# A gated causal convolution on one core: which load goes on which DMA queue at the start, and how the last left-over piece is evicted at the end

## The chip, the cores and the metric

The kernel runs on one core of one Trainium2 chip. The core has a matrix engine (TensorE, "PE" in the profile, with its weight loads as "PEld"), a vector engine (VectorE, "DVE"), a scalar engine (ScalarE, "ACT"), GpSimd ("POOL") and a queue engine (SyncE, "SP"). Transfers between the chip's memory and the core are issued here from two instruction streams, SP's and ACT's, and are carried out by 16 DMA engines. The metric is the device time of one execution in microseconds (us); 287.65 us is the median of three runs before the change.

## The reference

```python
B, T, D, K = (2, 16000, 256, 3)          # x: (B, T, D), w: (K, D, 2D), w_o: (D, D), all bf16
dil = 2
pad = (K - 1) * dil
xp = jnp.pad(x, ((0, 0), (pad, 0), (0, 0)))
h = jnp.einsum('btc,cd->btd', xp[:, pad:pad + T, :], w[0])
for i in range(1, K):
    off = pad - i * dil
    h = h + jnp.einsum('btc,cd->btd', xp[:, off:off + T, :], w[i])
f = h[..., :D]
g = h[..., D:]
z = jnp.tanh(f) * jax.nn.sigmoid(g)
return z @ w_o
```

Each output step t needs x at t, t-2 and t-4, each through its own 256 x 512 matrix ("tap" 0, 1, 2); half of the 512 results go through tanh, half through sigmoid, their product is `z` (called the gate below), and `z` goes through a 256 x 256 matrix.

## The kernel before

**Tiling.** Time is cut into rows of four steps (`j` = 0 to 3), 4000 rows per batch. Channels lie on the 128 partitions, in two halves `ct`. Rows are taken in 33 groups: 160 rows, then groups of 256 rows, and at the end 160, 128 and 128 rows. For each group there are four blocks of 128 output channels (`oi`, in the order of `O_ORDER`), so the main loop runs over `k = 4 * group + oi`, 132 steps. A step has two PSUM banks, `a` (steps 0 and 1 of each row) and `b` (steps 2 and 3).

**The two ways to form a step.** `direct` (L222) forms both banks tap by tap from the three weight matrices: 12 matmuls a step. It is used for the first group, steps 0 to 3, since it needs nothing but x and the taps. From step 4 on `products` (L201) needs 8 matmuls a step: two with mixed matrices `wm`, `wp` on a difference `mm` and a sum `pp` of x, two with tap 0 and two with tap 2 on differences `dd`. `weights` (L140) makes the mixed matrices: ACT halves tap 1 (L141), DVE adds taps 0 and 2 (L142) and forms `wm` and `wp` (L144). `pre_m`, `pre_p` and `pre_d` (L171, L177, L183) make `mm`, `pp` and `dd` on DVE and, for one quarter of group 1's `dd` and all later ones, GpSimd. `copy_m2` and `combine` (ACT L247, DVE L254 and L255) join the two banks, `activate` (ACT, L268) applies tanh or sigmoid, `gate` (DVE, L277) multiplies.

**Output.** `out_mm` (L281) multiplies a piece of `z` (up to 128 rows, two of the four steps of a row, called `jp` 0 or 1) by `w_o` into an `o_ps` bank of 128 x 512 values; `out_evict` (L295) copies that bank to the tile `osb` on ACT (L305) or, near the end, on DVE (L303), and after `jp` 1 issues the store of both `jp` from SP (L308). A piece is evicted one step after it was made (the list `made`), so one piece of the last but one group is left over when the loop ends: before the change it is evicted in the pass `k == NB`, on DVE, ahead of `finish`.

**The start.** The order is written out by hand. ACT's stream issues the load of tap 0 (`w0_sb`, L116) and then the load of its function table (L117). SP's stream issues x for the first 80 rows and the next 80 rows (L122, `xn0` and `xn1`, 160 KB each), then taps 1 and 2 (`w12_sb`, L126, 512 KB), then a transposing load of x for the second chunk (L104), the output matrix (L131) and another transposing load. PE meanwhile runs 24 matmuls on zeros (`warm_up`, L91), transposes `xn0` when it has landed (`turn(0)`, L155), runs 4 more zeros, transposes `xn1`, runs 4 zeros again and begins tap 0. `turn` copies each transposed half from PSUM to the tile `xt`, one half on DVE (L161), one on ACT (L163). The direct steps then run tap by tap: tap 0 of steps 0 to 2 (12 matmuls of 320 columns), tap 1, tap 2, and then step 3.

```python
    for tap in range(K):
        for k in range(3):
            direct(k, (tap,))
    weights()
```

**The end.** `finish` (L312) takes the last block of the last group: `activate`, two half gates (L322, first `jp` 1, then `jp` 0), and for each `jp` two banks of `z @ w_o` (L330); ACT copies the first bank (L335) and DVE the second (L337) to a tile `osb_end`, and SP stores it (L339).

Of the kernel before, what the change touches and what calls it, by code (L numbers as in the profile page):

```python
# [13 lines left out]
def kernel(  # L14
# [18 lines left out]
    nc = tc.nc  # L33
    bf16 = mybir.dt.bfloat16
    f32 = mybir.dt.float32
    B, T, D = x.shape
    K, _, D2 = w.shape
    P = 128
# [2 lines left out]
    NT = D // P  # L41
    RH = 16
    RG = 256
    N_WARM = (24, 4, 4)
    O_ORDER = (0, 2, 1, 3)
    FIRST = (160,)
    LAST = (128, 128)
# [40 lines left out]
    def warm_up(n):  # L88
        wps = ps_a.tile([P, 2 * RG], f32, name="a")
        for _ in range(n):  # L90
            nc.tensor.matmul(wps[:, :P], lhsT=warm[:], rhs=warm[:], start=True, stop=True)  # L91
# [20 lines left out]
    w0_sb = consts.tile([P, CT, D2], bf16)  # L112
    w12_sb = consts.tile([P, 2, CT, D2], bf16)
    wo_sb = consts.tile([P, NT, D], bf16)
    w_taps = [w0_sb, w12_sb[:, 0], w12_sb[:, 1]]
    nc.scalar.dma_start(out=w0_sb[:], in_=w[0].rearrange("(ct c) d -> c ct d", c=P))  # L116
    nc.scalar.preload_act_table(ACT.Sigmoid)  # L117
    warm_up(N_WARM[0])
    xns = []
    for i, (r0, r) in enumerate(TILES):  # L120
        xn = consts.tile([P, 4, D], bf16, name=f"xn{i}")
        nc.sync.dma_start(  # L122
            out=xn[:r], in_=x[0, 4 * r0:4 * (r0 + r), :].rearrange("(r j) c -> r j c", j=4)
        )
        xns.append(xn)
    nc.sync.dma_start(out=w12_sb[:], in_=w[1:3].rearrange("k (ct c) d -> c k ct d", c=P))  # L126
    ident = consts.tile([P, P], bf16)
    make_identity(nc, ident[:])
    for c in range(2):
# [18 lines left out]
    def turn(i):  # L148
        r0, r = TILES[i]
        for h in range(2):  # L150
            pool, tag = ((ps_o, "o_ps"), (ps_b, "b"))[i]
            tp = pool.tile([P, 2, CT, P], bf16, name="tp", tag=tag)
            for j in range(2):
                for ct in range(CT):
                    nc.tensor.transpose(  # L155
                        out=tp[:, j, ct, :r], in_=xns[i][:r, 2 * h + j, ct * P:(ct + 1) * P],
                        identity=ident[:r, :r],
                    )
            dst = xts[0][:, 2 * h:2 * h + 2, :, RH + r0:RH + r0 + r]
            if h == 0:  # L160
                nc.vector.tensor_copy(out=dst, in_=tp[:, :, :, :r])  # L161
            else:
                nc.scalar.copy(out=dst, in_=tp[:, :, :, :r])  # L163
# [7 lines left out]
    def pre_m(g):  # L171
        xp, yp, xc, yc = views(g)
        G = groups[g]
        G["m"] = m_pool.tile([P, 2, CT, RG], bf16, name="mm")
        return nc.vector.tensor_tensor(out=G["m"][:, :, :, :G["R"]], in0=xc, in1=yp, op=ALU.subtract)  # L175
# [25 lines left out]
    def products(k, which):  # L201
        g, oi = divmod(k, 4)
        G = groups[g]
        o = O_ORDER[oi]
        osl = slice(o * P, (o + 1) * P)
        R = G["R"]
        N = 2 * R
        if which in (1, 2):
            G["ab"[which - 1], oi] = (ps_a, ps_b)[which - 1].tile([P, 2 * RG], f32, name="ab"[which - 1])
        wmat, mv, bank, first = {  # L210
            2: (wm_sb, lambda ct: G["m"][:, :, ct, :R], "b", True),
            1: (wp_sb, lambda ct: G["p"][:, :, ct, :R], "a", True),
            3: (w_taps[0], lambda ct: G["d"][:, 2:4, ct, :R], "b", False),
            0: (w_taps[2], lambda ct: G["d"][:, 0:2, ct, :R], "a", False),
        }[which]
        for ct in range(CT):
            nc.tensor.matmul(  # L217
                G[bank, oi][:, :N], lhsT=wmat[:, ct, osl], rhs=mv(ct),
                start=first and ct == 0, stop=ct == CT - 1, skip_group_check=True,
            )  # L220
# [21 lines left out]
    def copy_m2(k):  # L242
        g, oi = divmod(k, 4)
        G = groups[g]
        N = 2 * G["R"]
        G["ss", oi] = ss_pool.tile([P, 2 * RG], f32, name="ss")
        nc.scalar.copy(out=G["ss", oi][:, :N], in_=G["b", oi][:, :N])  # L247
# [9 lines left out]
    def activate(k):  # L257
        g, oi = divmod(k, 4)
        G = groups[g]
        R = G["R"]  # L260
        o = O_ORDER[oi]
        if oi == 0:
            G["th"] = act_pool.tile([P, NT, 4, RG], bf16, name="th")
            G["sg"] = act_pool.tile([P, NT, 4, RG], bf16, name="sg")
            G["z"] = z_pool.tile([P, NT, 4, RG], bf16, name="zz")
        dst = G["th"][:, o] if o < NT else G["sg"][:, o - NT]
        for h, bank in ((1, "b"), (0, "a")):
            nc.scalar.activation(  # L268
                out=dst[:, 2 * h:2 * h + 2, :R],
                in_=G[bank, oi][:, :2 * R].rearrange("p (q r) -> p q r", q=2),  # L270
                func=ACT.Tanh if o < NT else ACT.Sigmoid,
            )
# [19 lines left out]
                    start=(dt == 0), stop=(dt == NT - 1),  # L292
                )

    def out_evict(g, rb0, jp, on_dve):  # L295
        G = groups[g]
        rn = min(P, G["R"] - rb0)
        ps = slice(rb0 - max(0, rb0 + rn - P), rb0 - max(0, rb0 + rn - P) + rn)
        if jp == 0:
            G["osb", rb0] = osb_pool.tile([P, 4, D], bf16, name="osb")  # L300
        osb, o_ps = G["osb", rb0], G["o", rb0, jp]
        if on_dve:
            nc.vector.tensor_copy(out=osb[ps, 2 * jp:2 * jp + 2, :], in_=o_ps[ps])  # L303
        else:
            nc.scalar.copy(out=osb[ps, 2 * jp:2 * jp + 2, :], in_=o_ps[ps])  # L305
        if jp == 1:
            t0 = 4 * (G["r0"] + rb0)
            nc.sync.dma_start(  # L308
                out=out[G["b"], t0:t0 + 4 * rn, :].rearrange("(p j) d -> p j d", j=4), in_=osb[ps]
            )  # L310

    def finish():  # L312

        g = NG - 1
        G = groups[g]
        R = G["R"]
        assert R <= P
        dt = NT - 1
        activate(4 * g + 3)
        for jp in (1, 0):  # L320
            js = slice(2 * jp, 2 * jp + 2)
            nc.vector.tensor_tensor(  # L322
                out=G["z"][:, dt, js, :R], in0=G["th"][:, dt, js, :R], in1=G["sg"][:, dt, js, :R], op=ALU.mult
            )
        for jp in (1, 0):
            osb = osb_pool.tile([P, 2, D], bf16, name="osb_end")
            for q in range(2):
                ps = (ps_a if q == 0 else ps_b).tile([P, 2 * RG], f32, name="ab"[q])
                for d in range(NT):
                    nc.tensor.matmul(  # L330
                        ps[:R, :D], lhsT=G["z"][:, d, 2 * jp + q, :R], rhs=wo_sb[:, d, :],
                        start=(d == 0), stop=(d == NT - 1),
                    )
                if q == 0:
                    nc.scalar.copy(out=osb[:R, q, :], in_=ps[:R, :D])  # L335
                else:
                    nc.vector.tensor_copy(out=osb[:R, q, :], in_=ps[:R, :D])  # L337
            t0 = 4 * G["r0"]
            nc.sync.dma_start(  # L339
                out=out[G["b"], t0:t0 + 4 * R, :].rearrange("(p j) d -> p j d", j=4)[:, 2 * jp:2 * jp + 2, :],  # L340
                in_=osb[:R],
            )
# [10 lines left out]
    NG = len(groups)  # L353
    NB = 4 * NG
    todo, made = [], []
    turn(0)
    warm_up(N_WARM[1])
    turn(1)
    warm_up(N_WARM[2])
    for tap in range(K):  # L360
# [21 lines left out]
    k = N_DIRECT + 1  # L382
    while k <= NB:
        g, oi = divmod(k, 4)
        if k < NB:
            products(k, 2)
            products(k, 1)
            copy_m2(k)
        products(k - 1, 3)
        products(k - 1, 0)  # L390

        for piece in made:
            out_evict(*piece, k == NB or g == NG - 1 and oi in (0, 2))
        made = []
        n = 1 if k < NB else 0
        while todo and todo[0][0] <= k and n:
            piece = todo.pop(0)[1]
            out_mm(*piece)
            made.append(piece)
            n -= 1  # L400

        if k < NB:
            combine(k)
        last = None
        if k < NB and oi == (1 if g == 1 else 0) and g + 1 < NG:
            last = pre_m(g + 1)
        elif k < NB and oi == 2 and g + 1 < NG:
            last = pre_p(g + 1)
        elif oi == 3 and g < NG:
            last = gate(g, 0)  # L410
        elif oi == 1 and 1 < g < NG:
            last = gate(g - 1, 1)
            drain(g - 1, k + 1)
        if k < NB and g + 1 < NG:
            pre_d(g + 1, oi, nc.gpsimd, last)
        if k < NB:
            activate(k - 1)

        if k < NB and oi == 3 and loaded < len(chunks) and groups[min(g + 1, NG - 1)]["chunk"] + 2 >= loaded:
            load_chunk(loaded)  # L420
            loaded += 1
        k += 1
    assert not todo and not made
    finish()


# [28 lines left out]
```

## Time and profile before

| what | us |
|---|---|
| median of three runs | 287.65 |
| lowest and highest of them | 287.0 and 288.33 |
| the profiled execution, its own time | 288.56 |
| span of the profiled execution, first to last instruction | 286.5 |
| PE busy in it | 281.1 |
| ACT busy in it | 261.1 |
| DVE busy in it | 241.8 |

All times of the trace count from the start of the span. The profiled execution is one run: its own time lies 0.91 us above the median and above the highest of the three. Start and length of an instruction are both printed; on ACT and DVE a following instruction can start a little before the one ahead has ended. Matmuls are printed by their start, and their ends are modelled. A name such as "ACTq" or "SPq" is the stream of instructions of that engine that issues transfers or waits for counters, as against the engine's own work. Of a transfer the profile has the time of its issue and the time until it has landed:

```
w_sb<-in_w_dram SPq DMA_DIRECT2D x1, 512.0 KB, 5.2
xn<-in_x_dram SPq DMA_DIRECT2D x2, 160.0 KB, 3.8
w_sb<-in_w_dram ACTq DMA_DIRECT2D x1, 256.0 KB, 4.1
xt<-in_x_dram SPq DMA_TRANSPOSE x2, 6.7
```

These are the issues in the first 15 us; the last number is the median from issue to landing.

### The profile page before, as it was taken

The numbers are of one execution on the slowest core, as the hardware profiler recorded it, in microseconds if no ns is written. First come the engines' busy times: TensorE is split into PE (matmuls) and PEld (weight loads), VectorE is DVE, ScalarE is ACT, GpSimd is POOL, SyncE is SP. The second block draws the span as 40 slices with busy tenths as digits, with TensorE's granted clock in tenths as the row PEclk, the third lists the DMA queues.
The fourth block names the chain that finished last, engine by engine and source line by source line (L and its number), as shares of the span: only waits on it lengthen the run. The fifth ranks groups of instructions, "written<-read, shape, count | busy, mean of one in ns | idle before, by whom it ended". The sixth has DMA issues, their size and how long they took to land.

```text
span 286.5 us, 4835 instructions
## 1 busy us (share of the span) xinstructions
PE 281.1 (98%) x1632; PEld 159.2 (56%) x1632; DVE 241.8 (84%) x401; ACT 261.1 (91%) x521; POOL 126.1 (44%) x133
## 2 busy tenths in 40 slices
PE   7999999999999999999999999999999999999994
PEld 6655555555555555555555555555555555555783
DVE  1788988888888888888888888888888888888885
ACT  3489999999999999999999999999999999999994
POOL 1134444454455455445445445445445544543430
PEclk9999999999999999999999999999999999999999
DMA  7908783561926429182371913718273251611222
GB/s 196 209 0 200 184 167 106 125 166 38 223 76 144 120 74 185 73 192 71 112 188 39 224 73 82 182 66 196 75 165 98 82 132 55 118 46 65 76 110 82
DMA packets 75767, 34.50 MB, mean 120 GB/s; under 512 B 66432, under 2 KB 67712, under 8 KB 75744
## 3 DMA queue, kind: packets, MB, share of 16 engines
q1 hardware_dynamic: 75472, 33.95, 46.3%
q8 instruction: 12, 0.20, 0.3%
q10 hardware_dynamic: 272, 0.26, 0.3%
q14 instruction: 11, 0.09, 0.1%
HBM read 1.25 MB, written 16.38 MB: 62 GB/s over the span
## 4 chain that ended last, share of the span: by engine, by line
PE 96%; DMA 2%; DVE 1%; issue 0%; SPq 0%; ACT 0%
PE b L217 37%; PE a L217 37%; PE o_ps L290 19%; DMA xn<-in_x_dram 2%; PE a L236 1%; PE b L236 1%; DVE osb_end L337 0%; PE tp L155 0%; DVE osb L303 0%; DVE a L255 0%; PE a L91 0%; DVE zz L277 0%; SPq L122 0%; ACT ss L247 0%; PE a L330 0%
## 5 line engine op out<-in xcount | busy, mean ns | idle before, releaser
L192 POOL TENSOR_TENSOR dd<-xt 128x512 bf16<-128x512 bf16 (+2 forms) x125 | 125.2, 1002 | 150.1 <-DVE zz L277 68.9
L254 DVE TENSOR_TENSOR b<-a,ss 128x512 f32<-128x512 f32 (+2 forms) x128 | 86.6, 676 | 35.2 <-ACT ss L247 32.7
L255 DVE TENSOR_TENSOR a<-a,ss 128x512 f32<-128x512 f32 (+2 forms) x128 | 85.3, 667 | 0.0
L247 ACT COPY ss<-b 128x512 f32<-128x512 f32 (+2 forms) x128 | 72.7, 568 | 12.5 <-PE b L217 0.9
L217 PEld LDWEIGHTS <-w_sb 128*128 128x128 bf16 x512 | 49.9, 98 | 55.9 <-DVE a L255 0.4
L290 PE MATMUL o_ps<-wo_sb,zz 128*128 128x256 bf16 x504 | 75.7, 273 | 0.0
L217 PE MATMUL a<-pp,wp_sb 128*128 128x512 bf16 (+2 forms) x256 | 73.8, 370 | 0.0
L217 PE MATMUL a<-dd,w_sb 128*128 128x512 bf16 (+2 forms) x256 | 73.8, 370 | 0.0
L217 PE MATMUL b<-mm,wm_sb 128*128 128x512 bf16 (+2 forms) x256 | 73.8, 370 | 0.0
L217 PE MATMUL b<-dd,w_sb 128*128 128x512 bf16 (+2 forms) x256 | 73.8, 370 | 0.0
L305 ACT CAST osb<-o_ps 128x512 bf16<-128x512 f32 (+1 forms) x123 | 72.9, 593 | 0.1
L290 PEld LDWEIGHTS <-zz 128*128 128x128 bf16 x504 | 49.1, 98 | 30.8 <-DVE zz L277 0.5
L268 ACT ACTIVATE th<-b 128x512 bf16<-128x512 f32 (+2 forms) x66 | 39.2, 594 | 3.9 <-PE b L236 3.8
L277 DVE TENSOR_TENSOR zz<-th,sg 128x1024 bf16<-128x1024 bf16 (+2 forms) x65 | 42.7, 658 | 0.0
L217 PEld LDWEIGHTS <-wp_sb 128*128 128x128 bf16 x256 | 25.0, 98 | 27.9
L268 ACT ACTIVATE sg<-b 128x512 bf16<-128x512 f32 (+2 forms) x66 | 39.3, 595 | 0.5 <-PE b L236 0.4
L268 ACT ACTIVATE sg<-a 128x512 bf16<-128x512 f32 (+2 forms) x66 | 39.3, 596 | 0.0
L268 ACT ACTIVATE th<-a 128x512 bf16<-128x512 f32 (+2 forms) x66 | 39.3, 595 | 0.0
L217 PEld LDWEIGHTS <-wm_sb 128*128 128x128 bf16 x256 | 25.0, 98 | 3.3
L175 DVE TENSOR_TENSOR mm<-xt 128x1024 bf16<-128x1024 bf16 (+2 forms) x32 | 21.2, 664 | 0.0
L181 DVE TENSOR_TENSOR pp<-xt 128x1024 bf16<-128x1024 bf16 (+2 forms) x32 | 21.2, 664 | 0.0
L236 PEld LDWEIGHTS <-w_sb 128*128 128x128 bf16 x48 | 5.2, 110 | 2.7
(29 smaller groups left out, 38.1 us busy)
## 6 DMA issues: line engine op xcount, KB each, us to landing
out_dram<-osb SPq DMA_DIRECT2D x61, 256.0 KB, 2.0
w_sb<-in_w_dram SPq DMA_DIRECT2D x1, 512.0 KB, 5.2
xn<-in_x_dram SPq DMA_DIRECT2D x2, 160.0 KB, 3.8
xt<-in_x_dram SPq DMA_TRANSPOSE x17, 6.6
w_sb<-in_w_dram ACTq DMA_DIRECT2D x1, 256.0 KB, 4.1
out_dram<-osb_end SPq DMA_DIRECT2D x2, 128.0 KB, 1.7
wo_sb<-in_w_o_dram SPq DMA_DIRECT2D x1, 128.0 KB, 3.5
out_dram<-osb SPq DMA_DIRECT2D x2, 64.0 KB, 1.9
```

The lines of the kernel that those rows point to most:

```text
L175: return nc.vector.tensor_tensor(out=G["m"][:, :, :, :G["R"]], in0=xc, in1=yp, op=ALU.subtract)
L181: return nc.vector.tensor_tensor(out=G["p"][:, :, :, :G["R"]], in0=xc, in1=yp, op=ALU.add)
L192: ins = eng.tensor_tensor(out=G["d"][:, j, :, :R], in0=a[:, q], in1=s[:, q], op=ALU.subtract)
L217: nc.tensor.matmul(G[bank, oi][:, :N], lhsT=wmat[:, ct, osl], rhs=mv(ct), start=first and ct == 0, stop=ct == CT - 1, skip_group_check=True,)
L236: nc.tensor.matmul(G[bank, oi][:, :2 * R], lhsT=w_taps[tap][:, ct, osl], rhs=mv[:, :, ct, :], start=tap == 0 and ct == 0, stop=tap == K - ...
L247: nc.scalar.copy(out=G["ss", oi][:, :N], in_=G["b", oi][:, :N])
L254: nc.vector.tensor_tensor(out=pb[:, :N], in0=pa[:, :N], in1=ss[:, :N], op=ALU.subtract)
L255: nc.vector.tensor_tensor(out=pa[:, :N], in0=pa[:, :N], in1=ss[:, :N], op=ALU.add)
L268: nc.scalar.activation(out=dst[:, 2 * h:2 * h + 2, :R], in_=G[bank, oi][:, :2 * R].rearrange("p (q r) -> p q r", q=2), func=ACT.Tanh if o ...
L277: return nc.vector.tensor_tensor(out=G["z"][:, dt, :, :R], in0=G["th"][:, dt, :, :R], in1=G["sg"][:, dt, :, :R], op=ALU.mult)
L290: nc.tensor.matmul(o_ps[:rb0 + rn - lo, q, :], lhsT=G["z"][:, dt, 2 * jp + q, lo:rb0 + rn], rhs=wo_sb[:, dt, :], start=(dt == 0), stop=(dt ...
L305: nc.scalar.copy(out=osb[ps, 2 * jp:2 * jp + 2, :], in_=o_ps[ps])
```

## The change

At the start tap 0 and taps 1 and 2 change places: SP's stream now issues x, x, tap 0; ACT's stream issues its table load first and taps 1 and 2 after it. The zeros between the two transposes go from 4 to 1 and those after them from 4 to 5. At the end the left-over piece is no longer evicted ahead of `finish`: it is evicted inside it, behind the two half gates, DVE copying one half of the bank and ACT the other. The last store is issued from ACT's stream in place of SP's.

```diff
-    N_WARM = (24, 4, 4)
+    N_WARM = (24, 1, 5)
...
-    nc.scalar.dma_start(out=w0_sb[:], in_=w[0].rearrange("(ct c) d -> c ct d", c=P))
     nc.scalar.preload_act_table(ACT.Sigmoid)
+    nc.scalar.dma_start(out=w12_sb[:], in_=w[1:3].rearrange("k (ct c) d -> c k ct d", c=P))
     warm_up(N_WARM[0])
...
-    nc.sync.dma_start(out=w12_sb[:], in_=w[1:3].rearrange("k (ct c) d -> c k ct d", c=P))
+    nc.sync.dma_start(out=w0_sb[:], in_=w[0].rearrange("(ct c) d -> c ct d", c=P))
...
-    def out_evict(g, rb0, jp, on_dve):
+    def out_evict(g, rb0, jp, by):
...
-        if on_dve:
-            nc.vector.tensor_copy(out=osb[ps, 2 * jp:2 * jp + 2, :], in_=o_ps[ps])
-        else:
-            nc.scalar.copy(out=osb[ps, 2 * jp:2 * jp + 2, :], in_=o_ps[ps])
+        if "D" in by:
+            q = slice(1 if "A" in by else 0, 2)
+            nc.vector.tensor_copy(out=osb[ps, 2 * jp + q.start:2 * jp + 2, :], in_=o_ps[ps, q])
+        if "A" in by:
+            q = slice(0, 1 if "D" in by else 2)
+            nc.scalar.copy(out=osb[ps, 2 * jp:2 * jp + q.stop, :], in_=o_ps[ps, q])
...
-    def finish():
+    def finish(left):
...
+        for piece in left:
+            out_evict(*piece, "AD")
         for jp in (1, 0):
...
-            nc.sync.dma_start(
+            (nc.sync if jp == 1 else nc.scalar).dma_start(
                 out=out[G["b"], t0:t0 + 4 * R, :].rearrange("(p j) d -> p j d", j=4)[:, 2 * jp:2 * jp + 2, :],
                 in_=osb[:R],
             )
...
-        for piece in made:
-            out_evict(*piece, k == NB or g == NG - 1 and oi in (0, 2))
-        made = []
+        if k < NB:
+            for piece in made:
+                out_evict(*piece, "D" if g == NG - 1 and oi in (0, 2) else "A")
+            made = []
...
-    finish()
+    finish(made)
```

In the changed program ACT's half of the left-over piece stands behind a wait on DVE's counter at the value that DVE's own half raises it to, so it starts only when DVE's half is done; SP's store of that piece waits for ACT's half.

More of the change, by code (lines that the diff above doesn't have):

```diff
@@ L422 @@
         k += 1
-    assert not todo and not made
-    finish()
+    assert not todo
+    finish(made)
 _INS = ['x', 'w', 'w_o']
```

## The prediction

> **What bounds the kernel now.** I read the page, the chain of waits at both ends, the timeline of the first 20 and the last 6 us, and the busy time by stretches. The page and the first pieces of the chain:
>
> ```profile
> PE 281.1 (98%) x1632; PEld 159.2 (56%) x1632; DVE 241.8 (84%) x401; ACT 261.1 (91%) x521; POOL 126.1 (44%) x133
> ```
>
> ```profile
> 1.20 4.33 DMA xn<-in_x_dram
> 5.58 0.71 PE tp L155 x8
> 6.29 0.43 PE a L91 x4
> 6.72 0.53 PE a L236 x2
> ...
> 8.85 0.44 PE a L236 x2
> 9.29 0.27 PE b L236 x2
> ```
>
> From 6.72 to about 281.5 PE is never out of work, so only what comes before 6.72, PE's pace just after it, and the tail can change. The second x load lands at 5.53 and sets the start of tap 0. Up to 8.85 a pair of matmuls takes 0.53, later 0.27 to 0.28: four pairs at the slow pace lose 4 x 0.26 = 1.03. The timeline has the issues and what hangs on taps 1 and 2:
>
> ```profile
> 0.73 0.45 ACTq L116 DMA_DIRECT2D w_sb<-in_w_dram  x1
> 0.73 0.87 SPq L122 DMA_DIRECT2D xn<-in_x_dram  x2
> 1.21 1.28 ACT L117 ACT_TABLE_LOAD   x1 [1.21 <-PEq L439]
> 1.65 0.42 SPq L126 DMA_DIRECT2D w_sb<-in_w_dram  x1
> ...
> 6.97 1.23 DVE L142 TENSOR_TENSOR wt_sb<-w_sb 128x1024 f32<-128x1024 bf16 x1 [0.59 <-DMA w_sb<-in_w_dram]
> ...
> 12.98 1.04 POOL L192 TENSOR_TENSOR dd<-xt 128x512 bf16<-128x512 bf16 x1 [11.61 <-DVE dd L192]
> ```
>
> Landings follow from issue plus the times of the transfers: x at 4.04 and 5.5, tap 0 at 0.73 + 4.1 = 4.83, taps 1 and 2 at 1.65 + 5.2 = 6.87. In the stretches of time, DMA moves 350 GB/s between 3 and 4 us, with x and tap 0 in flight together:
>
> ```profile
> 3.00:4.00 1.00, 0.73 (x7) 0.46 (x5) 0.00 (x0) 0.00 (x0) 0.00 (x0) 1.00 1.11 350
> ```
>
> The tail: DVE's eviction of the left-over piece (L303) stands ahead of the half gates (L322).
>
> ```profile
> 281.44 0.68 DVE L303 CAST osb<-o_ps 128x512 bf16<-128x512 f32 x1
> 281.65 0.38 ACT L268 ACTIVATE sg<-a 128x256 bf16<-128x256 f32 x1
> 282.04 0.48 DVE L322 TENSOR_TENSOR zz<-th,sg 128x256 bf16<-128x256 bf16 x2
> ...
> 282.70 0.81 ACT L335 CAST osb_end<-a 128x256 bf16<-128x256 f32 x2 [0.68 <-PE a L330]
> ...
> 282.92 0.86 DVE L337 CAST osb_end<-b 128x256 bf16<-128x256 f32 x2 [0.40 <-PE b L330]
> ...
> 283.41 0.81 SPq L339 DMA_DIRECT2D out_dram<-osb_end  x2
> ```
>
> **The change part by part**, against the profiled execution (288.56; span 286.5 and 2.06 around it).
>
> *x earlier.* Tap 0's 262 KB no longer fly beside x. At 350 GB/s they are 0.75 us, so the second x lands at 4.78; if it came as soon after its issue as the first did (3.3), at 1.16 + 3.3 = 4.46. I take 4.55, nearer the second, since then no other load is under way. The 8 transposes (0.71) and 5 zeros (5 x 0.107, from 24 in 2.56) end at 5.84. The copy of the last transposed half before ended 0.47 after the transposes, so the zeros hide it. Gain on 6.72: 0.9.
>
> *Tap 0 third on SP.* Issued at 1.65 in place of 0.73. With 3.3 to 4.33, the two x landings, it lands between 4.95 and 5.98. The zeros cover it to 5.84; beyond, at most 0.15 is lost. I take nothing; floor of the gain 0.7.
>
> *Taps 1 and 2 behind the table load.* If ACT's stream stands still while the table loads, the issue starts at 0.73 + 1.28 + 0.03 = 2.04 and lands at 2.04 + 5.2 = 7.24. Tap 0's 12 matmuls at 0.137 need 1.64, so tap 1 begins at 7.5 at the earliest: hidden, by 0.25. DVE's chain from L142 to the end of GpSimd's `dd` (6.97 to 14.02, 7.05 long) then ends at 14.4; the products that read it stand at 16.64 in the chain now and would come at 14.7 with both gains: hidden by 0.3. Behind the transposing load, which now follows the small tap 0 on SP and competes, taps 1 and 2 could take that load's 6.3 to 6.9 and land at 8.9.
>
> By the Trainium skill, "DMA: Bandwidth & Descriptors", section "Issuing engines are not separate DMA queues", the queues share the same 16 engines and only issue time is saved. The 350 GB/s for two queues agrees. By that rule all 1.1 MB land no sooner than now; only their order changes, and the sum stays.
>
> *PE's pace.* No row shows what makes the pace change at 8.85. Bound: if PE without its idle 0.32 and 0.39 (3.73 to 4.04, 5.19 to 5.58) runs fast from 5.84, the 1.03 goes; if the change still comes at 8.85, the slow stretch grows from 2.13 to 3.05 and half of that growth, 0.46, is lost. I take the middle, -0.28, for nothing says which end is nearer. The clock falls again after the work ends (0.54 is the mean of that half microsecond):
>
> ```profile
> 285.50:286.00 0.50, 0.00 (x0) 0.00 (x0) 0.00 (x0) 0.00 (x0) 0.00 (x0) 0.54 0.00 0
> ```
>
> The Trainium skill, "TensorE: Matmul & The Clock Gate", Part 1, says that the clock is decided at the ends of free-running windows of 3.413 us, full speed after a busy one. The rows agree: full speed at about 9.0 and half from 285.54 lie some 276.5 apart, 81 such windows. By it, which end holds differs from run to run; Part 4 of that page adds that transposes do not count fully as work, which speaks for the loss.
>
> *Fewer and more zeros.* 4 + 4 become 1 + 5, two less, in the times above already.
>
> *The tail.* Without L303 ahead, the first half gate starts at 281.77, when `sg` of bank b is done (281.37 + 0.38), and the second at 282.05 behind `sg` of a. DVE's half of the left-over piece (0.42, as one L337) runs 282.30 to 282.72. ACT's half waits for it by the program's order: 282.75 to 283.12, and behind it in ACT's stream wait both L335 copies, which before began at 282.70. ACT starts 256-wide work every 0.28 (281.37, 281.65), so they start at 283.03 and 283.31 and end at 283.68; DVE's L337 end at 283.5. The last store goes at 283.71 instead of 283.81. But the left-over piece's 262 KB leave SP at 283.15, not 282.2, and now fly beside both last stores: at 350 GB/s the 524 KB from about 283.95 (issue plus 0.8, as the store of 282.2 shows DMA from 283.0) end at 285.45, where the last one landed at 283.81 + 1.7 = 285.5 before. Bounds: -0.1 (issue plus 1.7), +0.7 (268 GB/s as between 284.5 and 285.0, and 0.3 to land). I take +0.2: 285.45 plus some of that.
>
> *Sum.* -0.9 - 0.28 + 0.2 = -0.98: 287.58 against the profiled 288.56. That run lies 0.91 above the median, so 286.65 for a median run.
>
> **The rivals.**
>
> *ACT's stream does not wait for the table load* (the change doesn't do what it says; slower). Then taps 1 and 2 are issued at 0.76 and 512 KB, not 256, fly beside x. Second x: 5.5 to 5.7. Tap 0, last behind x, lands when all has come through, as taps 1 and 2 did: 1.65 + 5.2 = 6.87. Tap 0 starts at 6.9 instead of 6.72, PE's pace gains nothing and may lose 0.3: +0.2 to +0.5, and the tail +0.2: 288.2. For it: ACT's issuing stream does run ahead of ACT's work; here it is at a wait at 101.2, before the ACTIVATE ahead of that wait has begun:
>
> ```profile
> L247 ACTq EVENT_SEMAPHORE  x2: 866/866/866, 101.2 to 103.4; - x2
> ```
>
> ```profile
> 101.40 0.62 ACT L268 ACTIVATE sg<-a 128x512 bf16<-128x512 f32 x1
> ```
>
> Against it: the table load began 0.03 after the issue ahead of it ended (1.18 to 1.21), as close as two issues on SP follow each other (1.60 to 1.65), while DVE's first work needed 0.13 after its release at 0.69. That looks like work of the stream itself. It decides over 0.5% only if tap 0 lands past 7.9. The Trainium skill, "Perfetto Trace Analysis", section "Sequencer Loop", has engine instructions pushed to a queue while the stream reads on, "rarely" with work in the stream itself: its main rule is this rival.
>
> *Both idle gaps close and PE is fast from tap 0 on.* -0.9 - 1.03 + 0.2 = -1.73; with the offset 285.9. For it: x at about 3.7 and 4.55 leaves PE hardly idle. Against: the profiled run lies 0.91 above the median, and if a longer slow stretch is part of that, a median run has less to gain.
>
> *Taps 1 and 2 late.* At 8.9 tap 1 waits; DVE's chain ends at 9.0 + 7.05 = 16.05, 0.6 before the 16.64 of now. Start -0.6, tail +0.2: -0.4; 287.2. For it: the transposing load in the same engines; against: its issue too begins at 2.1, and 512 KB take 1.5 us at 350 GB/s.
>
> **How the numbers follow.** Forecast 0.36, own range 286.1 to 287.2; ACT's stream not waiting 0.30; fast from tap 0 0.22; taps 1 and 2 late 0.12. 0.5% of 287.65 is 1.44, about what a measurement of this kernel can tell from no change: faster lies under 286.2, slower over 289.1. Faster: 0.2 of the forecast and 0.8 of the fast case, 0.25. Slower: 0.25 of the case that does not wait and little of the rest, 0.1. Same: 0.65. The range goes from 285.4, the fast case and some of its spread, to 288.7, ACT's stream not waiting with its upper 0.5 and the tail's upper end.
>
> **What would show it.** The issue of taps 1 and 2 on ACT's stream at 2.04 or at 0.76 decides first. Then: second x at about 4.55; tap 0's first matmul near 5.85; no wait of PE at tap 1; the pair length dropping before 8.85 or not; half gates at 281.77 less the gain; ACT's half after DVE's; the last store landing 1.7 to 2.2 after its issue. The forecast is wrong if the ACT issue is at 0.76, or if any load but x sets tap 0.

## The result, and the profile after

The change makes the kernel slower: 289.61 us (median of 22 runs, 287.75 to 291.59) against 288.40 for the kernel before (22 runs, 286.64 to 290.37). The ratio is 1.0057, 95% interval 1.0039 to 1.0076. The forecast was 286.65 us, 1.0 less than before, in a range of 285.4 to 288.7; the measured median lies above the range. Of the kernel before, the three runs known at the prediction had a median of 287.65, which is 0.75 below that of the 22.

The profiled execution after took 291.59 us, its span is 288.7. The page's first lines:

```profile
span 288.7 us, 4832 instructions
...
PE 281.9 (98%) x1630; PEld 159.7 (55%) x1630; DVE 241.6 (84%) x401; ACT 261.1 (90%) x522; POOL 126.1 (44%) x133
```

The span is 2.2 us longer; the busy times are the same within 0.8. This run is the slowest of its 22, 1.98 above their median, and the profile before, at 288.56, lies near the 22 runs' median, so the two profiles lie farther apart than the medians, which differ by 1.21. To see where the 2.2 us lie, cut the span at two matmuls that both kernels have: the first of `products` (step 4) and the last of the main loop. From the one to the other both take 267.50 us. Before the first it is 13.77 and now 15.58: 1.8 us. After the last it is 5.21 and now 5.59: 0.4 us. Nothing in between moved.

The start, from the timeline of the changed kernel (start, length, engine, line, instruction, and in brackets the idle time before it with what ended it):

```profile
0.73 1.28 ACT L116 ACT_TABLE_LOAD   x1 [0.73 <-PEq L444]
...
0.74 0.87 SPq L122 DMA_DIRECT2D xn<-in_x_dram  x2
0.76 0.47 ACTq L117 DMA_DIRECT2D w_sb<-in_w_dram  x1
...
1.66 0.42 SPq L126 DMA_DIRECT2D w_sb<-in_w_dram  x1
...
4.08 0.31 PE L91 MATMUL a<-warm 128*128 128x128 bf16 x1
...
6.05 0.72 PE L155 MATMUL tp<-ident,xn 80*128 80x80 bf16 x8 [1.67 <-DMA xn<-in_x_dram]
```

The load of taps 1 and 2 stands behind the table load in the program, yet it is issued at 0.76, while the table load runs from 0.73 to 2.01. It goes out with the first x, and 0.4 us ahead of the second x. The second x lands at 6.0 in place of 5.53, and PE, with one zero matmul in place of four to run meanwhile, stands idle for 1.67 us. The chain of waits shows what follows:

```profile
1.20 4.80 DMA xn<-in_x_dram
6.01 0.05 issue
6.05 0.72 PE tp L155 x8
6.77 0.53 PE a L91 x5
7.30 0.53 PE a L236 x2
...
12.10 0.35 PE b L236 x2
12.45 0.28 PE a L236 x2
```

Tap 0 starts at 7.30 in place of 6.72 (0.58 later), and PE's pace changes near 12.1 in place of 8.85. Nine pairs of matmuls run at 0.53 and a tenth partly, instead of four. The other 1.2 of the 1.8 us at the start is this, in these two runs; the medians share out otherwise, as the experiments show.

The tail of the changed kernel, same columns:

```profile
283.44 0.38 ACT L268 ACTIVATE sg<-a 128x256 bf16<-128x256 f32 x1
283.58 0.57 DVE L324 TENSOR_TENSOR zz<-th,sg 128x256 bf16<-128x256 bf16 x2 [0.25 <-ACT sg L268]
...
284.06 0.42 DVE L304 CAST osb<-o_ps 128x256 bf16<-128x256 f32 x1
...
284.52 0.37 ACT L307 CAST osb<-o_ps 128x256 bf16<-128x256 f32 x1 [0.69 <-DVE osb L304]
284.79 0.66 ACT L339 CAST osb_end<-a 128x256 bf16<-128x256 f32 x2
285.36 0.37 SPq L343 DMA_DIRECT2D out_dram<-osb_end  x1
285.47 0.36 ACTq L343 DMA_DIRECT2D out_dram<-osb_end  x1
```

The half gates no longer wait for the eviction, but ACT's half waits 0.69 for DVE's, and the last copy and the last store wait behind it. The last two stores need 2.0 and 2.2 us from issue to landing, where both needed 1.7 before.

### The profile page after: what moved, and what is told of

It is laid out like the page before. It is cut to its first block, busy times and chain, and to the rows that moved or that the text cites. A ratio compares the mean times of both kernels' runs of the same rounds, so it can differ in the third digit from the quotient of the medians.

```text
span 288.7 us, 4832 instructions
## 1 busy us (share of the span) xinstructions
PE 281.9 (98%) x1630; PEld 159.7 (55%) x1630; DVE 241.6 (84%) x401; ACT 261.1 (90%) x522; POOL 126.1 (44%) x133
## 3 DMA queue, kind: packets, MB, share of 16 engines
HBM read 1.25 MB, written 16.38 MB: 61 GB/s over the span
## 4 chain that ended last, share of the span: by engine, by line
PE 96%; DMA 2%; ACT 0%; DVE 0%; SPq 0%; issue 0%
PE b L217 37%; PE a L217 37%; PE o_ps L290 19%; DMA xn<-in_x_dram 2%; PE a L236 2%; PE b L236 2%; PE tp L155 0%; ACT osb_end L339 0%; PE a L91 0%; DVE osb L304 0%; SPq L122 0%; ACT sg L268 0%; ACT osb L307 0%; DVE zz L324 0%
## 5 line engine op out<-in xcount | busy, mean ns | idle before, releaser
L217 PEld LDWEIGHTS <-w_sb 128*128 128x128 bf16 x512 | 50.0, 98 | 55.9 <-DVE a L255 0.4
L236 PEld LDWEIGHTS <-w_sb 128*128 128x128 bf16 x48 | 5.7, 120 | 3.4
```

Source lines behind the costliest of these rows:

```text
L217: nc.tensor.matmul(G[bank, oi][:, :N], lhsT=wmat[:, ct, osl], rhs=mv(ct), start=first and ct == 0, stop=ct == CT - 1, skip_group_check=True,)
L236: nc.tensor.matmul(G[bank, oi][:, :2 * R], lhsT=w_taps[tap][:, ct, osl], rhs=mv[:, :, ct, :], start=tap == 0 and ct == 0, stop=tap == K - ...
```

## The experiments

The ten experiments were timed in three sets, each set on one chip together with the kernel before. In the first (start alone, end alone, held behind the table load, zeros 28, 8, 4) the kernel before has a median of 288.61, in the second (one queue, idle time filled, zeros with the new end, two banks) of 287.90, in the third (store on SP, one queue with two banks) of 287.73. A ratio is against the set's own runs; medians of different sets are comparable only to a few tenths. The table has, for the profiled execution of each, where the granted clock goes to full speed, the start of tap 0 and of the first `products` matmul, the time from the last main matmul to the end (tail), all in us, then the median of the timed runs and the ratio.

| run | full speed at | tap 0 | first product | tail | median | ratio, 95% interval |
|---|---|---|---|---|---|---|
| before | 9.06 | 6.51 | 13.77 | 5.21 | | 1 |
| after | 12.14 | 7.10 | 15.58 | 5.59 | 289.61 | 1.0057 (1.0039 to 1.0076) |
| start alone | 12.52 | 7.35 | 15.89 | 5.24 | 289.45 | 1.0025 (0.9997 to 1.0053) |
| end alone | 9.55 | 6.38 | 13.95 | 5.61 | 287.40 | 0.9982 (0.9950 to 1.0015) |
| held behind the table load | 4.86 | 5.06 | 12.71 | 5.59 | 287.57 | 0.9963 (0.9936 to 0.9991) |
| one queue | 5.23 | 5.37 | 11.77 | 5.22 | 286.75 | 0.9967 (0.9945 to 0.9989) |
| zeros 28, 8, 4 | 6.09 | 6.35 | 12.45 | 5.24 | 287.14 | 0.9942 (0.9911 to 0.9973) |
| after, idle time filled | 6.54 | 6.97 | 13.00 | 5.60 | 287.94 | 1.0003 (0.9980 to 1.0026) |
| zeros, new end | 4.75 | 6.35 | 12.36 | 5.62 | 287.31 | 0.9984 (0.9963 to 1.0004) |
| zeros, new end, store on SP | 6.62 | 6.30 | 12.47 | 5.55 | 287.11 | 0.9968 (0.9940 to 0.9996) |
| zeros, new end, two banks | 6.21 | 6.26 | 12.32 | 5.21 | 286.92 | 0.9955 (0.9935 to 0.9975) |
| one queue, two banks | 5.74 | 5.51 | 12.31 | 5.24 | 286.84 | 0.9957 (0.9927 to 0.9988) |

The kernel before differs by up to 3.9 us from run to run (286.58 to 290.48 in the 33 runs of the first set), so ratios against it are only good to some 0.3%. Starts and tails of the profiles, and medians of kernels that differ little from run to run, tell more.

**Start alone, end alone.** The change was cut in two.

```diff
-    N_WARM = (24, 4, 4)
+    N_WARM = (24, 1, 5)
-    nc.scalar.dma_start(out=w0_sb[:], ...)
     nc.scalar.preload_act_table(ACT.Sigmoid)
+    nc.scalar.dma_start(out=w12_sb[:], ...)
...
-    nc.sync.dma_start(out=w12_sb[:], ...)
+    nc.sync.dma_start(out=w0_sb[:], ...)
```

> Only the start of the change: tap 0 and taps 1 and 2 change places, zeros 24, 1, 5; the end is that of the kernel before. Theory A (taps 1 and 2, issued at 0.76 beside the table load, hold up the second x, PE stands idle for 1.7 us and its pace changes one window later): second x near 6.0, tap 0 near 7.1 to 7.3, about 1.2 us slower than before, ratio near 1.004. Theory B (the end is what costs): ratio 1.000 to 1.001.

> Only the end of the change: left-over piece by halves behind the gates, last store from ACT's stream; start as before. Theory A: the tail is 0.4 us longer (5.3 from the last main matmul to the end before, 5.7 after), ratio near 1.0015. Theory B (the end is what costs): ratio 1.004 or more.

The start alone has its first product at 15.89 and the old tail; the end alone has the old start and a tail of 5.61. Start and tail of the whole change, 15.58 and 5.59, are thus those of its halves, within 0.3. The start alone has a median of 289.45, 0.84 above the kernel before; its interval, 0.9997 to 1.0053, holds theory A's 1.004 and just holds theory B's 1.000, so the profile decides here more than the time. The end alone came out at 0.998, whose interval holds both 1.0015 and its opposite: this comparison could not tell 0.4 us in a kernel whose start varies by more, and the end was tested again below.

**Held behind the table load, and one queue.** The first makes the changed kernel do what its order suggests: a one-column ACT copy behind the table load, and the load of taps 1 and 2 made to wait for it.

```diff
     nc.scalar.preload_act_table(ACT.Sigmoid)
-    nc.scalar.dma_start(out=w12_sb[:], ...)
+    tick = consts.tile([P, 1], bf16)
+    seen = nc.scalar.copy(out=tick[:], in_=warm[:, :1])
+    held = nc.scalar.dma_start(out=w12_sb[:], ...)
+    tc.add_manual_dep(held.ins, seen.ins.name, ...)
```

> The changed kernel, but the load of taps 1 and 2 waits for a one-column ACT copy that stands behind the table load, so its issue comes near 2.3 in place of 0.76. Theory A: second x lands near 4.5, tap 0 starts near 5.9, PE has no idle time over 0.3 us, taps 1 and 2 land near 7.5; about 0.9 to 1.9 us better at the start, 0.4 lost at the end: ratio 0.995 to 0.999. Rival (the 16 engines are shared, so the order of issue does not matter): second x near 6.0 as in the changed kernel, ratio 1.005.

Its timeline:

```profile
2.25 0.45 ACTq L119 DMA_DIRECT2D w_sb<-in_w_dram  x1
...
4.16 0.74 PE L162 MATMUL tp<-ident,xn 80*128 80x80 bf16 x8
...
5.06 0.43 PE L243 MATMUL a<-xt,w_sb 128*128 128x320 bf16 x2
...
8.32 0.45 PE L243 MATMUL a<-xt,w_sb 128*128 128x320 bf16 x2 [1.39 <-DMA w_sb<-in_w_dram]
```

With the issue at 2.25 the second x lands at 3.8, 2.2 us sooner than in the changed kernel, its transposes start at 4.16, PE does not stand idle before tap 0, and tap 0 starts at 5.06 at full speed. The rival, by which the order of issue does not matter, is out. Then PE waits 1.39 us for taps 1 and 2, which take 6.0 us from issue to landing, with the transposing load issued just before them: they land at 8.28, between the forecast's 7.24 and the 8.9 of the prediction's third rival.

The other puts all four loads on SP, in the order x, x, tap 0, taps 1 and 2, with zeros 24, 1, 5 and the old end.

```diff
-    nc.scalar.dma_start(out=w0_sb[:], ...)
...
+    nc.sync.dma_start(out=w0_sb[:], ...)
     nc.sync.dma_start(out=w12_sb[:], ...)
```

> The kernel before with all four first loads on SP in the order x, x, tap 0, taps 1 and 2, and zeros 24, 1, 5; the end is that of the kernel before. Theory A (what is issued early in bytes beside x holds up x): second x near 4.2, tap 0 starts near 5.1, taps 1 and 2 land near 6.9 with the transposing load behind them and not beside them, first product at step 4 near 11.4, median near 286.1, ratio near 0.991. Rival (taps 1 and 2 cannot land sooner than in the run that waited for the table load, 8.28): first product near 12.7, ratio near 0.995.

```profile
w_sb<-in_w_dram SPq DMA_DIRECT2D x1, 512.0 KB, 5.2
xn<-in_x_dram SPq DMA_DIRECT2D x2, 160.0 KB, 2.7
```

These are its issues and the median time to landing. x now lands 2.7 us after issue in the median of its two loads (3.8 in the kernel before), and taps 1 and 2 at 2.12 + 5.2 = 7.3, a microsecond sooner than in the run before this, so PE waits only 0.16 at tap 1. The first product came at 11.77, not 11.4, and 0.2 us more were lost behind it: DVE's chain from L142 starts at 7.41 and PE waits for `mm` and `pp`. The median of 286.75 is 0.65 above that of theory A; the rival named no median, but its first product was 1.3 later, which makes about 287.4. The ratio, 0.9967, misses theory A's 0.991 and is above the rival's 0.995 too, since more runs of the kernel before were near 286.8 in this set (its median here 287.90, in the first set 288.61). What rules the rival out is the landing, 7.3 against its 8.28.

**Zeros before, and idle time filled.** These change no load. One fills PE's gaps in the kernel before, the other the large gap of the changed kernel.

```diff
-    N_WARM = (24, 4, 4)
+    N_WARM = (28, 8, 4)
...
-    N_WARM = (24, 1, 5)
+    N_WARM = (24, 19, 5)
```

> The kernel before with zeros 28, 8, 4 in place of 24, 4, 4, which fill PE's two idle gaps at the start and change nothing else. If PE's idle time decides when its pace changes: the pace changes in more runs before tap 0 is through, 0.3 to 0.8 us faster in the mean, ratio 0.997 to 0.999. If the idle time does not matter: the zeros that outlast the landing cost 0.1 to 0.3 us, ratio 1.000 to 1.001.

> The changed kernel with 19 zeros in place of 1 between the two transposes, which fill PE's idle time before the second x (1.7 to 2.0 us) and leave every load as it is. Theory A, with the idle time as what puts the pace off: second x still near 6.0 to 6.3, tap 0 near 7.1 to 7.4, but the pace changes before tap 0 starts in most runs; median near 288.3, ratio near 0.9985, and no runs above 289. Rival (the late x alone costs): ratio as the changed kernel, 1.005.

The chain of the first of them, the kernel before with zeros 28, 8, 4:

```profile
4.79 0.85 PE a L91 x8
5.65 0.55 PE tp L155 x8
6.20 0.23 PE a L91 x4
6.43 0.35 PE a L236 x2
6.79 0.36 PE b L236 x2
7.15 0.27 PE a L236 x2
```

and of the changed kernel with its idle time filled:

```profile
4.26 2.03 PE a L91 x19
6.29 0.46 PE tp L155 x8
6.75 0.28 PE a L91 x5
7.03 0.37 PE a L236 x2
```

In both the pairs run at 0.27 to 0.3 from the second or third on. Eight more zero matmuls take the kernel before to 287.14 with all ten runs between 286.62 and 287.26, where the 33 runs of before, beside it, reach 290.48. Its shortest runs were as short already (286.58); the long ones are gone. That is more than was expected: 1.35 us in the mean, not 0.3 to 0.8. In the changed kernel the second x is as late as ever (transposes at 6.08), and filling the wait takes the median from 289.61 to 287.94 (two sets; the ratio goes from 1.0057 to 1.0003). Theory A had 288.3 and no run above 289; the highest is 288.57.

Set against 287.14 for the old loads with filled gaps, the rest is 0.8 us: 0.55 at the first product (13.00 against 12.45) and 0.36 in the tail, which makes 0.91. The run with zeros 28, 8, 4 and the new end, shown below, is a closer match, from the same set and with the same end: 287.31 against 287.94, so the late x alone costs 0.63 (first product 12.36 against 13.00). The slow pace costs far more, 1.67 by these medians, but the kernel before pays most of that too: 288.61 against 287.14 with its gaps filled, 1.47. So of the 0.84 us that the start alone lost, about 0.6 is the late x and the rest PE's pace; by the means of the same runs, 1.19 lost, it is about half and half. How much the pace adds is thus known only to 0.2 to 0.6 us.

**The end again, on the steady start.** Three kernels with zeros 28, 8, 4: the new end; the same with the last store on SP again; the same with the second half of the left-over piece in another PSUM bank, which takes away what makes ACT's half wait for DVE's.

```diff
-            (nc.sync if jp == 1 else nc.scalar).dma_start(
+            nc.sync.dma_start(
...
         G["o", rb0, jp] = o_ps
+        banks = [o_ps[:, 0, :], o_ps[:, 1, :]]
+        if split:
+            G["o2", rb0, jp] = ps_a.tile([P, 2 * RG], f32, name="a")
+            banks[1] = G["o2", rb0, jp][:, :D]
```

> The kernel before with zeros 28, 8, 4 and the end of the change. Its start hardly differs from run to run, so the end shows alone: theory A says that the tail is 5.6 us from the last main matmul against 5.24, and the median 0.35 to 0.4 us above the run with zeros 28, 8, 4 and the old end, near 287.5, ratio near 0.9955. Rival (the end is no slower, as the run with the changed end alone had a ratio of 0.998): median 287.1 or less.

> The kernel before with zeros 28, 8, 4 and the end of the change, but the last store issued from SP again. If the ACT stream is no worse for the last store than SP: it goes out 0.1 to 0.3 us later behind SP's other stores, tail 5.6 to 5.8, median 287.3 to 287.5. If a store from ACT's stream lands late (2.2 us after its issue against 1.7 on SP before): tail 5.2 to 5.4, median near 287.1.

> As the run with zeros 28, 8, 4 and the end of the change, but the two halves of the left-over piece lie in two PSUM banks, so that ACT's half does not wait for DVE's. If that wait is what makes the end slow: ACT's half starts with the end of its last sigmoid, the last two stores leave 0.3 to 0.4 us earlier, tail 5.2 to 5.3, median near 287.15. If it is the left-over store's bytes, which fly beside the last two stores: tail 5.5, median near 287.4.

Two timelines side by side, the new end and then the new end with two banks:

```profile
280.85 0.42 DVE L304 CAST osb<-o_ps 128x256 bf16<-128x256 f32 x1
...
281.30 0.37 ACT L307 CAST osb<-o_ps 128x256 bf16<-128x256 f32 x1 [0.69 <-DVE osb L304]
...
281.70 0.34 SPq L310 DMA_DIRECT2D out_dram<-osb  x1
...
282.25 0.36 ACTq L343 DMA_DIRECT2D out_dram<-osb_end  x1
```

```profile
280.46 0.38 ACT L314 CAST osb<-o_ps 128x256 bf16<-128x256 f32 x1
...
280.81 0.42 DVE L309 CAST osb<-a 128x256 bf16<-128x256 f32 x1
...
281.29 0.34 SPq L317 DMA_DIRECT2D out_dram<-osb  x1
...
282.16 0.36 ACTq L350 DMA_DIRECT2D out_dram<-osb_end  x1
```

With two banks ACT's half starts 0.84 sooner, the left-over store leaves 0.41 sooner, and the tail is 5.21, that of the old end. So the wait costs the new end its 0.4. The medians agree: 287.31 with the wait, 286.92 without, in one set (287.14 for the old end comes from another). The last store itself does not leave 0.3 to 0.4 earlier, as was expected, but only 0.09, of which 0.04 is an earlier last main matmul; most of the gain is that it lands 1.90 us after its issue, not 2.25. Why it lands sooner was not tested by itself. The rows fit the left-over store, which flies beside it: with 0.55 us between the two issues the last store takes 2.25, with 0.87 (two banks) 1.90, with 0.92 (last store on SP) 1.87, with 1.65 (old end) 1.75.

The stream of the last store matters little: from ACT it is issued 0.37 us sooner behind the last main matmul than from SP, but lands at the same distance from it, 4.64 and 4.63. The tail is 5.55 on SP, 5.62 on ACT; the medians, 287.11 and 287.31, come from two sets of runs, and this 0.2 is not settled; the run fits neither of its two expectations whole. Nor does the new end's 287.31 meet either expectation, near 287.5 or at most 287.1; it is the tails, and the two medians of one set, that show the cost of the end.

**Both together.** One queue and two banks.

> All four first loads on SP in the order x, x, tap 0, taps 1 and 2, zeros 24, 1, 5, and the end of the change with the left-over piece in two PSUM banks. By theory A the two halves add: start as with one queue (first product at step 4 near 11.8), tail 5.2: median near 286.7, ratio near 0.995, no better than the one-queue run with the old end, for that end has the same tail. Rival (the end with two banks is worth more than its tail shows): median 286.5 or less.

286.84, as expected: not better than one queue alone. In its profile taps 1 and 2 landed at 7.84, half a microsecond later than in the other run with one queue, with the same program at that place. So of the microsecond between 8.28 and 7.3 above, half can be the difference from run to run.

## Why the prediction was wrong

*The step that failed is "Taps 1 and 2 behind the table load"*: "If ACT's stream stands still while the table loads, the issue starts at 0.73 + 1.28 + 0.03 = 2.04". It was issued at 0.76. The row that spoke for standing still was the 0.03 between ACT's issue and the table load in the profile before. It showed how soon a table load starts behind an issue, not whether an issue waits behind a table load. The row against it, ACT's stream waiting at 101.2 for work that had not yet begun, was the right one to go by. By the Trainium skill, "Perfetto Trace Analysis", section "Sequencer Loop", the stream reads on, and the trace agrees, 0.76 against 2.01 for the end of the table load.

In the sum this breaks the term "x earlier", -0.9: the second x was to land at 4.55 and landed at 6.0, and tap 0 started 0.58 later, not 0.9 sooner. That is 1.5 of the 2.2 us between the forecast change of -0.98 and the measured +1.21. The tail is 0.2 of it, and the remaining 0.5 falls to the pace, forecast at -0.28. The median lies outside the range also because the base was low: 0.75 us lie between the three runs of before and the 22.

*What took its place was the first rival, with 0.30, and its price was too small.* It gave 288.2. Its parts: second x 5.5 to 5.7, measured 6.0; tap 0 landing at 6.87, measured 1.66 + 4.9 = 6.56, and not what PE waited for; tap 0's start 6.9, measured 7.30 in the chain. The reason is that I let the two queues share evenly. In the packet records 79 of the 80 packets of the second x begin after 4.25, when 442 of the 512 of taps 1 and 2 have begun. A load issued 0.4 us sooner on the other queue went ahead almost whole; whether the earlier issue or the other queue put it ahead, no run here separates. In the kernel before it is the same: 231 of tap 0's 256 packets begin before 3.75, and 70 of the second x's 80 after it.

*That rival's "PE's pace gains nothing and may lose 0.3" fell short in the profiled run*, where the pace lost 1.2; against the 0.2 to 0.6 us that the timed runs give, 0.3 was about right. I had bounded the loss with a change of pace at 8.85, as before. The two records of the granted clock in the changed kernel, full at 12.14 and half at 288.62, lie 276.48 apart, as before; in the runs where they lie farther apart it is 279.89, 3.41 more. These are 81 and 82 times 3.413, which agrees with the Trainium skill, "TensorE: Matmul & The Clock Gate", Part 1, on a free-running window. Now count back from full speed in steps of 3.413. In the kernel before, both gaps of PE, 0.71 together, lie in the stretch that ends at 5.65, and full speed came at the next end, 9.06. In the changed kernel the idle time, 4.38 to 6.05, reaches into two stretches, 0.93 of it into the one that ends at 5.31 and 0.74 into the one that ends at 8.72, and full speed came at the end of the third, 12.14. Whether transposes count fully as work, as the prediction quoted against the gain, no run here settles.

*With the load held back, x and tap 0 came sooner than the forecast's terms, and the cover failed.* The second x, forecast at 4.55, landed at 3.8; tap 0, near 5.85, started at 5.06, at full speed since 4.86, which the forecast had left to its rival. But taps 1 and 2 landed at 8.28 and not at 7.24, and the cover named for them, tap 0's 12 matmuls, was too short by 1.39. The ratio, 0.9963, is close to the forecast's 0.9965 only by luck, because these misses cancel.

*The tail* was predicted at +0.2 with bounds of -0.1 and +0.7; it is +0.4. The mechanism was as written: gates sooner, ACT's half behind DVE's, the left-over store late beside the last two. What was mis-sized is the landing, 2.2 us after the last issue. *The middle*, predicted to be untouched, is 267.50 in both.

*The offset to the median.* I treated the profiled run's 0.91 above the median as a constant. The 22 runs of before show two groups, 286.6 to 287.7 and 288.3 and up, and the profile is of a run with a late change of pace. The spans of the 33 runs in the first set fall into three groups, 284.6 to 285.1, 286.2 to 287.0 and 288.0 to 288.4, about 1.7 us apart; one more stretch of 3.413 at half pace would cost 1.71, an estimate. The time outside the span is not constant either: 2.06 in the profile before, 2.89 in the one after.

## What to carry to other kernels

A place behind an engine instruction in the same stream did not hold a load back: it was issued 1.25 us before the table load ahead of it had ended, and only a wait held it. If a transfer must stay out of another's way, try it behind that one on the same queue, as with one queue here. Idle time of the matrix engine before its first real work cost twice, once as waiting and once through a later change to full speed. Zero matmuls that fill it are a cheap repair: they alone gave 0.6% (ratio 0.9942, 0.9911 to 0.9973). When work is split between two engines, look up in the built program whether one half waits for the other; two halves of one PSUM bank, here also one tile, did; two banks, here two tiles, did not.

## What the runs showed of the hardware

A table load of 1.28 us on ACT and the issue of a transfer from ACT's stream run side by side (0.73 and 0.76). Of two loads on different queues, the one issued 0.4 us sooner had begun 442 of its 512 packets before the other had begun more than one of its 80. The two plain x loads of 160 KB landed 2.6 us after issue each with the load of taps 1 and 2 held back, 2.3 and 3.2 with all loads on one queue, and the second took 4.8 in the changed kernel, with 512 KB of another queue ahead of it. The moment of full clock differs from run to run: 4.75, 6.09, 6.21 and 6.62 in four profiles with the same start. In the eight profiles in which PE's waits from 0.99 to tap 0 add up to 0.33 us or less, it was never later than 6.62; in the other four, with 0.58 us or more, it was 9.06 to 12.52.
